# One more group solved whole on VectorE, its Y turned without TensorE, and the weights' low parts subtracted on GpSimd

## The chip, the cores and the metric

The kernel runs on one core of one Trainium2 chip. The metric is the device time of one execution in microseconds (us). Three timed executions of the kernel before took 637.04 to 637.57 us, with a median of 637.5 us.

A core has five engines that run side by side and wait for one another through semaphores: PE (TensorE, matrix products and the loading of their weights), DVE (VectorE), ACT (ScalarE), POOL (GpSimd) and SP (here only the DMA issues). Each engine takes its own instructions strictly in the order in which the program lists them.

## The reference

A linear-attention recurrence (a delta rule) over 768 tokens, for 4 batches of 8 heads of size 48, feeds a gated two-layer network:

```python
k_n = k / (norm(k) + 1e-6)
for t in range(768):
    y[t] = q[t] @ state
    state = state + b[t] * outer(k_n[t], v[t] - state.T @ k_n[t])   # per batch and head
x = y.transpose(0, 2, 1, 3).reshape(3072, 384)
out = (sigmoid(x @ w_gate) * (x @ w_val)) @ w_out                   # 384 -> 1536 -> 384
```

Everything is float32, and the products of the network are made of pairs of narrower parts: each weight and each activation is split into a high part in a narrower float (fp32r) and a low part, the remainder.

## The kernel before

**Groups.** The 768 tokens are cut into 12 groups (g = 0 to 11) of 64 tokens. For one group and all 32 heads the recurrence becomes block algebra. Step by step:

- `gram` (L282): PE multiplies the keys with each other (`pg`); ACT copies the blocks out into `G` and `L`.
- `norms` (18 short DVE instructions): the norms of the keys and the factors `gam` and `mq` from the diagonal of `G`. `scale_v` (ACT, L279) scales V.
- The solve: a triangular 32 x 32 system for each of the chunks. `solve` (L329) does it whole on DVE: 31 pairs of a multiply (L347) and an add (L350), and a 32 x 32 transposition into `mt` (L352). `solve_halves` (L373) solves two 16 x 16 halves on DVE (15 pairs, L392 and L395) and joins them on PE with 64 small products `pz` and 64 small products `pm` (both L409), a DVE transposition (L422), an ACT copy (L423) and a DVE subtraction (L430); it needs `joint` (a cleared tile, GpSimd) and `lower_left` (ACT). Groups 0, 1 and 2 use the halves, the groups from 3 on the whole solve.
- `rest`, `updates` (three steps), `rows`, `advance`: PE products with the running state `su`, with ACT and DVE moving the results out of PSUM. `rows` leaves the group's Y in `ys`.
- Y has to be turned (tokens along the free axis) and split into `xh` and `xl` (the high and the low part of x) before the network can use it. `flip` (L533, groups 0 to 2) does it on PE (three transpositions `pt` for each half, L542), with ACT (L547) for the high and DVE (L548) for the low part. `turn` (L551, groups from 3 on) uses one DVE transposition (`yt`, L557), sixteen block copies, eight on GpSimd and eight on ACT (L562), one ACT cast for `xh` (L571) and one DVE subtraction for `xl` (L573).

**The network.** For each group and each f = 0 to 11: `gate_val` (PE, 24 products of both weights; L583 for group 0 in full float32, L586 with split parts from group 1 on), `gated` (ACT sigmoid L591, DVE multiply L592), `split_hi` and `split_lo` (ACT L597, DVE L602), and `outp` (PE, L611 or L617) two tiles later. From group 1 on, the products of `gate_val` go in the order high times high, high weight times `xl`, low weight times `xh`; so the second product of a group needs `xl`.

**The weights.** 36 weight pieces (three for each f) come in over DMA as 64-bit words, are put together (ACT L189 and L191, DVE L203) and split for the groups from 1 on: `weight_hi` (ACT cast, L212) writes the high part, `weight_lo` (DVE, L219) the low part. Memory is reused: the tile that `weight_hi` of an odd piece n writes is the one whose old content `weight_hi` and `weight_lo` of the pieces n - 3 and n - 2 read, so the odd cast n waits for the low part n - 2.

**The order.** `slot(s)` (L811) writes the order by hand. An even slot is a `gate_val` and an odd one an `outp`; 24 slots are one group of the network. In each slot run, in this order: the products, what the table `plan` holds for it, the split or the gating, what `late` holds, and what `tail` holds (the weight splits). Group g + 1 is solved and updated in the slots of group g. A tile below is called by group and f: (1,9) is `gate_val` of group 1 with f = 9 and what belongs to it, in slot 24 + 18 = 42.

Of the kernel before, what the change touches and what calls it, by code (L numbers as in the profile page):

```python
# [12 lines left out]
F32 = mybir.dt.float32  # L13
# [6 lines left out]
ALU = mybir.AluOpType  # L20
# [11 lines left out]
CP = 2 * J  # L32
# [23 lines left out]
def deltanet_gated_mlp(ctx: ExitStack, tc: tile.TileContext, kd, qd, kv, beta, words, out):  # L56
    nc = tc.nc
# [4 lines left out]
    wk = ctx.enter_context(tc.tile_pool(name="wk", bufs=1))  # L62
# [18 lines left out]
    joints = {0: scratch, 1: scratch}  # L81
# [25 lines left out]
    def load_q(g, after=None):  # L107
        for e in range(2):
            ins = nc.sync.dma_start(kqp[g % 2][64 * e:64 * e + 64, 2 + e:4 + e].rearrange("p s c t -> p (s c t)"), qd[g, e])
            pace(ins, after)  # L110
# [104 lines left out]
    def weight_lo(n):  # L215
        f, w = pieces[n]
        t, u = parts[w, f]
        parts[w, f] = t
        nc.vector.tensor_tensor(out=t[:, 1], in0=u, in1=t[:, 0].bitcast(F32), op=ALU.subtract)  # L219

    def joining():
        for n in range(len(pieces)):
# [88 lines left out]
    def masked(g):  # L311

        kq = kqp[g % 2]
        pool, tag = (ps_aux, "aux") if g else (ps_out, "po")
        pp = [pool.tile([128, J, C], F32, name=f"pp_{g}_{e}", tag=tag) for e in range(2)]
        for j in range(J):
            for e, x in KINDS:
                r, t = 64 * e, tokens_at(e, x)
                nc.tensor.matmul(out=pp[e][t:t + 64, j], lhsT=kq[r:r + D, x, j], rhs=kq[r:r + D, 3 if x else 2 + 2 * e, j], start=True, stop=True)  # L319

        def masks():
            for e, x in sorted(KINDS):
                t, sec = tokens_at(e, x), 5 if x else 2 + 2 * e
                nc.vector.tensor_tensor(out=kq[t:t + 64, sec], in0=pp[e][t:t + 64],  # L324
                                        in1=pmask[t:t + 64, e].unsqueeze(1).to_broadcast([64, J, C]), op=ALU.mult)
                yield
        return masks()
# [27 lines left out]
    def lower_left(g):  # L355

        if g == 0:
            for r in range(4):
                q, o = slice(32 * r, 32 * r + 32), 32 * (r % 2)
                nc.scalar.activation(wide[q, :, o:o + 16].rearrange("q c t -> q t c"), state[g]["G"][q, 0:16], AF.Copy, scale=under[q])  # L360
            return
        a = joints[g][:, 0]
        return nc.scalar.activation(a[:, :, 0:16].rearrange("q c t -> q t c"), state[g]["G"][:, 0:16], AF.Copy, scale=under)

    def joint(g):
        joints[g] = wk.tile([128, 3, CP, 32], F32, name=f"scratch_{g}", tag=f"xx{(g + 1) % 2}", bufs=1)
        nc.gpsimd.memset(joints[g][:, 0], 0.0)

    def clear(g):
        state[g]["X"] = X = wk.tile([128, 16, 32], F32, name=f"X_{g}", tag="X", bufs=1)  # L370
        nc.gpsimd.memset(X, 0.0)
# [258 lines left out]
    plan = collections.defaultdict(list)  # L630
    late = collections.defaultdict(list)

    def steps(gen, n=1):
        def fn():
            for _ in range(n):
                next(gen, None)
        return fn

    def spread(gen, total, lo, hi, room=lambda s: 1.0, into=plan):

        done, upto, whole = 0, 0.0, sum(room(s) for s in range(lo, hi))
        for s in range(lo, hi):
            upto += total * room(s) / whole
            n = total if s == hi - 1 else round(upto)
            into[s].append(steps(gen, n - done))
            done = n

    def chain(*gens):
        for q in gens:
            yield from q  # L650

    def take(gen, n=1):
        for _ in range(n):
            next(gen, None)

    def scaling(g, s):
        for i in range(4):
            plan[s + i].append(steps(scalings[g], 4))

    scalings = [scale_v(g) for g in range(N)]  # L660
    NORMS, SOLVE, HALVES = 18, 66, 40
# [78 lines left out]
    for part in (1, 0):  # L740
        plan[{1: 6, 0: 11}[part]].append(lambda part=part: load_rows(2, part))
    plan[13].append(lambda: load_q(2))
    halves2 = solve_halves(2)
    plan[12].append(lambda: clear(2))
    plan[23].append(lambda: joint(2))
    plan[24].append(lambda: lower_left(2))

    busy = collections.Counter()

    def mask_later(g, s):  # L750
        def fn():
            masks = masked(g)
            take(masks, 2)
            plan[s + 1].insert(0, steps(masks, 2))
        late[s].append(fn)
        for i in range(2):
            busy[s + i] += 1.4

    def gram_later(g, s):
        def fn():  # L760
            copies = gram(g)
            for i, n in enumerate((4, 2, 4) if g < 4 else (6, 4)):
                plan[s + 1 + i].append(steps(copies, n))
        late[s].append(fn)

    solves = []
    for g in range(N):
        w = W * (g - 1)
        if g == 0:
            late[3].append(lambda: advance(0))  # L770
            continue
        up, at_rows = (13, 19) if g < 3 else (9, 15)
        at_rest = {1: 8, 2: 28}.get(g, w + 6)
        late[at_rest].append(lambda g=g: rest(g))
        for step in range(3):
            late[w + up + 2 * step].append(lambda g=g, step=step: updates(g, step))
        late[w + at_rows].append(lambda g=g: rows(g))
        if g > 2:
            turned = turn(g)
            late[w + at_rows].append(steps(turned))  # L780
        late[w + at_rows].append(lambda g=g: advance(g))
        if g < 3:
            for c in range(2):
                late[w + at_rows + 2].append(lambda g=g, c=c: flip(g, c))
                busy[w + at_rows + 2] += 0.6
        else:
            for at, n in ((16, 3), (17, 3), (18, 2), (19, 1), (20, 1)):
                late[w + at].append(steps(turned, n))
            busy[w + 15] += 0.6
            busy[w + 20] += 0.6  # L790
        busy[at_rest] += 1.1
        busy[w + up + 2] += 1.1
        busy[w + at_rows] += 1.1
        busy[w + at_rows + 1] += 1.1
        if g == 1:
            mask_later(1, 14)
        else:
            if g > 2:
                plan[w - 27].append(lambda g=g: load_group(g))
            gram_later(g, {2: 3, 3: 32}.get(g, w - 18))  # L800
            mask_later(g, {2: 25, 3: 38}.get(g, w - 13))
            if g > 2:
                solves.append((g, w - 13 if g == 3 else w - 15, w + 8))
            scaling(g, {2: 25, 3: 43}.get(g, w - 4))
    spread(chain(norms(2), halves2), NORMS + 36, 8, 25, lambda s: max(0.1, 1.6 - busy[s]))
    for at in (26, 29, 30, 30, 31):
        plan[at].append(steps(halves2))
    for g, lo, hi in solves:
        spread(chain(norms(g), solve(g)), NORMS + SOLVE, lo, hi, lambda s: max(0.1, 1.6 - busy[s]))

# [71 lines left out]
```

## Time and profile before

| what | value |
|---|---|
| median of three timed runs | 637.5 us |
| the profiled execution's own time | 635.61 us |
| its span, first to last instruction | 633.9 us |
| PE busy | 614.6 us (97%) |
| DVE busy | 476.8 us (75%) |
| ACT busy | 344.0 us (54%) |
| POOL busy | 39.6 us (6%) |
| granted TensorE clock | 0.998 of full |

The profile shows one execution. Line numbers are those of the kernel before. An instruction's row gives its start, its duration, its engine and line, what it writes and reads, and in brackets how long the engine stood idle just before it and what ended that idle time. Durations of instructions that follow each other on an engine overlap a little, so the distance from start to start is shorter than the printed duration.

### The profile page before, as it was taken

What the parts mean: (1) busy time and instruction counts of PE and PEld (TensorE: products, weight loads), DVE (VectorE), ACT (ScalarE), POOL (GpSimd) and SP (SyncE); (2) the same over time, 40 slices, a digit from 0 to 9 for tenths busy, and PEclk for the clock granted to TensorE, in tenths of its full rate; (3) what the DMA queues carried; (4) which work ended last, traced back from release to release, by engine and by line L of the source; (5) the groups of instructions that cost most, each with busy time, mean ns of one, the idle gap of its engine ahead of it and who ended that gap; (6) DMA issues with size and microseconds to landing.
All of it is one profiled execution on the core that took longest, in us unless ns stands there. A gap on an engine that the chain in (4) does not pass through costs nothing.

```text
span 633.9 us, 24057 instructions
## 1 busy us (share of the span) xinstructions
PE 614.6 (97%) x10494; PEld 571.2 (90%) x10502; DVE 476.8 (75%) x1443; ACT 344.0 (54%) x933; POOL 39.6 (6%) x102
## 2 busy tenths in 40 slices
PE   6689999999999999999999999999999999999996
PEld 4367778989999999999999999999999999999996
DVE  5888897589977977977977977977987977953221
ACT  4879865567356356356355355355455455445222
POOL 6000000000002002002002002002002002001000
PEclk9999999999999999999999999999999999999999
DMA  9495831202203203103102102102112100100101
GB/s 271 177 296 181 277 91 54 53 2 87 52 3 86 52 4 86 42 12 86 45 11 86 34 21 87 27 28 86 26 29 86 26 4 3 26 3 2 26 1 25
DMA packets 17769, 41.06 MB, mean 65 GB/s; under 512 B 4224, under 2 KB 7296, under 8 KB 17664
## 3 DMA queue, kind: packets, MB, share of 16 engines
q1 hardware_dynamic: 17664, 39.53, 21.5%
q8 instruction: 82, 1.34, 0.9%
q14 instruction: 23, 0.19, 0.1%
HBM read 34.80 MB, written 4.72 MB: 62 GB/s over the span
## 4 chain that ended last, share of the span: by engine, by line
PE 91%; DVE 5%; ACT 1%; issue 1%; DMA 1%; ACTq 0%; SPq 0%; DVEq 0%
PE gv L586 45%; PE po L617 22%; PE gv L583 5%; PE pu L477 3%; PE po L611 3%; PE yy L503 2%; PE yy L506 2%; PE pk L446 2%; PE pg L291 2%; PE pp L319 2%; PE pd L524 2%; PE pk L469 1%; PE pm L409 1%; ACT su L483 1%; DVE kqp L324 1%
## 5 line engine op out<-in xcount | busy, mean ns | idle before, releaser
L586 PE MATMUL gv<-xx,w 128*128 128x256 f32 x2376 | 311.2, 285 | 0.0
L586 PEld LDWEIGHTS gv<-xx,w 128*128 128x128 f32 x2376 | 298.8, 191 | 3.1
L617 PE MATMUL po<-w,h 128*128 128x384 f32 x792 | 161.9, 340 | 0.0
L617 PEld LDWEIGHTS po<-w,h 128*128 128x128 f32 x792 | 133.8, 188 | 0.8
L597 ACT CAST h<-sg 128x256 fp32r<-128x256 f32 x132 | 53.5, 405 | 120.1 <-DVE sg L592 119.0
L591 ACT ACTIVATE sg<-gv 128x256 f32<-128x256 f32 x144 | 54.7, 380 | 107.8 <-PE gv L586 98.5
L592 DVE TENSOR_TENSOR sg<-sg,gv 128x256 f32<-128x256 f32 x144 | 60.1, 417 | 67.3 <-ACT sg L591 66.5
L350 DVE TENSOR_TENSOR X<-X,tmp 128x126 f32<-128x126 f32 (+22 forms) x279 | 71.1, 255 | 8.3
L347 DVE TENSOR_TENSOR tmp<-X,gp 128x126 f32<-128x126 f32 (+22 forms) x279 | 71.0, 254 | 8.3
L602 DVE TENSOR_TENSOR h<-sg,h 128x256 fp32r<-128x256 f32 x132 | 56.4, 428 | 13.2 <-ACT h L597 13.2
L562 POOL COPY x<-yt 32x192 f32<-32x192 f32 x72 | 28.3, 393 | 450.3 <-DVE yt L557 447.6
L279 ACT ACTIVATE kv<-kv,mq 128x48 f32<-128x48 f32 x192 | 47.9, 324 | 0.0
L483 ACT COPY su<-pu 32x384 f32<-32x384 f32 x92 | 43.3, 470 | 5.9 <-PE pu L477 4.1
L583 PE MATMUL gv<-xx,u 128*128 128x256 f32 x144 | 33.8, 385 | 0.7 <-issue 0.4
L324 DVE TENSOR_TENSOR kqp<-pp,pmask 64x512 f32<-64x512 f32 x48 | 32.3, 687 | 2.1 <-PE pp L319 1.1
L303 ACT COPY G<-pg 32x256 f32<-32x256 f32 (+1 forms) x69 | 25.3, 367 | 14.0 <-PE pg L291 12.7
L583 PEld LDWEIGHTS gv<-xx,u 128*128 128x128 f32 x144 | 26.6, 190 | 5.8 <-issue 0.8
L557 DVE STREAM_TRANSPOSE yt<-ys 128x768 f32<-128x768 f32 x9 | 8.8, 979 | 25.4 <-ACT ys L512 25.4
L457 DVE TENSOR_TENSOR R<-kv,pk 128x384 f32<-128x384 f32 x44 | 22.3, 549 | 6.6 <-PE pk L469 6.5
L562 ACT COPY x<-yt 32x192 f32<-32x192 f32 x72 | 25.2, 349 | 1.2
L212 ACT CAST w<-u 128x384 fp32r<-128x384 f32 x36 | 18.0, 508 | 8.1 <-DVE w L219 8.0
L531 DVE TENSOR_TENSOR su<-su,pd 48x384 f32<-48x384 f32 x40 | 21.7, 543 | 0.8 <-PE pd L524 0.4
(109 smaller groups left out, 556.2 us busy)
## 6 DMA issues: line engine op xcount, KB each, us to landing
raw<-in_words_dram SPq DMA_DIRECT2D x36, 384.0 KB, 5.5
kv<-in_kv_dram SPq DMA_DIRECT2D x24, 384.0 KB, 4.5
kqp<-in_qd_dram SPq DMA_DIRECT2D x24, 256.0 KB, 4.1
kqp<-in_kd_dram SPq DMA_DIRECT2D x24, 192.0 KB, 3.5
out_dram<-ot SPq DMA_DIRECT2D x48, 96.0 KB, 2.2
beta<-in_beta_dram SPq DMA_DIRECT2D x12, 16.0 KB, 4.0
```

What stands on the lines that cost most here:

```text
L279: nc.scalar.activation(V[:, c], V[:, c], AF.Copy, scale=mq[:, c, 0:1])
L347: nc.vector.tensor_tensor(out=tmp, in0=X[:, k:16, j:j + 1].to_broadcast([128, n, j]), in1=gp[:, j:j + 1, 0:j].to_broadcast([128, n, j]), o ...
L350: nc.vector.tensor_tensor(out=X[:, k:16, 0:j], in0=X[:, k:16, 0:j], in1=tmp, op=ALU.add)
L483: nc.scalar.copy(su[r:r + 32, 3 if x else e], pu[0][r:r + 32])
L562: copy(x[32 * q:32 * q + 32, :, :, a].rearrange("q k c s -> q c k s"), yt[32 * a:32 * a + 32, :, q::4])
L583: nc.tensor.matmul(out=pg[:, o], lhsT=parts[w, f][:, k * 128:(k + 1) * 128], rhs=x[0][:, k], start=k == 0, stop=k == KC - 1)
L586: nc.tensor.matmul(out=pg[:, o], lhsT=parts[w, f][:, a, k * 128:(k + 1) * 128], rhs=x[b][:, k], start=(k == 0 and q == 0), stop=(k == KC - ...
L591: nc.scalar.activation(h, st["gv", f][:, 0], AF.Sigmoid)
L592: nc.vector.tensor_tensor(out=h, in0=h, in1=st["gv", f][:, 1], op=ALU.mult)
L597: nc.scalar.copy(hh[:, 0], st["sg", f])
L602: nc.vector.tensor_tensor(out=hh[:, 1], in0=st["sg", f], in1=hh[:, 0].bitcast(F32), op=ALU.subtract)
L617: nc.tensor.matmul(out=po[s], lhsT=hh[:, a, ts], rhs=parts["o", f][:, w], start=(f == 0 and q == 0), stop=(f == NF - 1 and q == 2))
```

## The change

Three things. `weight_lo` runs on GpSimd instead of DVE, for all 36 pieces. Group 2 is solved by `solve` in place of `solve_halves`, over the slots 8 to 33; its cleared tile, its `lower_left` and the 128 small PE products go away. Group 2's Y is turned by `turn` in place of `flip`, and its updates and rows stand two slots earlier (35, 37, 39 and 41 in place of 37, 39, 41 and 43). A few steps of groups 2 and 3 move by one or two slots with it.

```diff
@@ weight_lo
-        nc.vector.tensor_tensor(out=t[:, 1], in0=u, in1=t[:, 0].bitcast(F32), op=ALU.subtract)
+        nc.gpsimd.tensor_tensor(out=t[:, 1], in0=u, in1=t[:, 0].bitcast(F32), op=ALU.subtract)
...
-    def joint(g):
-        joints[g] = wk.tile([128, 3, CP, 32], F32, name=f"scratch_{g}", tag=f"xx{(g + 1) % 2}", bufs=1)
-        nc.gpsimd.memset(joints[g][:, 0], 0.0)
...
-    halves2 = solve_halves(2)
-    plan[12].append(lambda: clear(2))
-    plan[23].append(lambda: joint(2))
-    plan[24].append(lambda: lower_left(2))
...
-        up, at_rows = (13, 19) if g < 3 else (9, 15)
+        up, at_rows = {1: (13, 19), 2: (11, 17)}.get(g, (9, 15))
...
-        if g > 2:
+        if g > 1:
             turned = turn(g)
             late[w + at_rows].append(steps(turned))
...
-        if g < 3:
+        if g < 2:
             for c in range(2):
                 late[w + at_rows + 2].append(lambda g=g, c=c: flip(g, c))
...
-            for at, n in ((16, 3), (17, 3), (18, 2), (19, 1), (20, 1)):
-                late[w + at].append(steps(turned, n))
+            for at, n in ((1, 3), (2, 3), (3, 2), (4, 1), (5, 1)):
+                late[w + at_rows + at].append(steps(turned, n))
...
-            gram_later(g, {2: 3, 3: 32}.get(g, w - 18))
-            mask_later(g, {2: 25, 3: 38}.get(g, w - 13))
-            if g > 2:
-                solves.append((g, w - 13 if g == 3 else w - 15, w + 8))
-            scaling(g, {2: 25, 3: 43}.get(g, w - 4))
-    spread(chain(norms(2), halves2), NORMS + 36, 8, 25, lambda s: max(0.1, 1.6 - busy[s]))
-    for at in (26, 29, 30, 30, 31):
-        plan[at].append(steps(halves2))
+            gram_later(g, {2: 3, 3: 31}.get(g, w - 18))
+            mask_later(g, {2: 25, 3: 36}.get(g, w - 13))
+            solves.append((g, *{2: (8, 34), 3: (35, 56)}.get(g, (w - 15, w + 8))))
+            scaling(g, {2: 24, 3: 44}.get(g, w - 4))
```

What this does to the order is seen at three places. The numbers at the end of a tile's name only tell tiles apart; `w_35` is weight piece 35, `sg_1_10` belongs to tile (1,10). The changed file is four lines shorter from `joint` on, so L558 there is L562 here, L567 is L571, L569 is L573, and L587, L588, L593 and L598 are L591, L592, L597 and L602.

ACT, in the last slots of the network's group 1, before:

```order
L279 ACTIVATE kv_3_1706<-kv_3_1706,mq_3_2495 128x48 x4
L597 CAST h_1_9_2616<-sg_1_9_2596 128x256
L512 COPY ys_2_2668<-yy_2_0_2618 128x8x48
L512 COPY ys_2_2668<-yy_2_1_2619 128x8x48
L279 ACTIVATE kv_3_1706<-kv_3_1706,mq_3_2495 128x48 x4
L591 ACTIVATE sg_1_10_2737<-gv_1_10_2710 128x256
L279 ACTIVATE kv_3_1706<-kv_3_1706,mq_3_2495 128x48 x4
L597 CAST h_1_10_2761<-sg_1_10_2737 128x256
L547 CAST xx_2_2763<-pt_2_0_2764 128x3x128
L547 CAST xx_2_2763<-pt_2_1_2770 128x3x128
L279 ACTIVATE kv_3_1706<-kv_3_1706,mq_3_2495 128x48 x4
L591 ACTIVATE sg_1_11_2807<-gv_1_11_2776 128x256
```

and now, from behind the sigmoid of tile (1,9) and three block copies on:

```order
L212 CAST w_34_2599<-u_17_1586 128x384
L212 CAST w_35_2602<-u_17_1586 128x384
L593 CAST h_1_9_2618<-sg_1_9_2583 128x256
L558 COPY x_2_2586<-yt_2_2519 32x2x3x32 x3
L279 ACTIVATE kv_3_1705<-kv_3_1705,mq_3_2439 128x48 x4
L587 ACTIVATE sg_1_10_2655<-gv_1_10_2624 128x256
L558 COPY x_2_2586<-yt_2_2519 32x2x3x32 x2
L279 ACTIVATE kv_3_1705<-kv_3_1705,mq_3_2439 128x48 x4
L593 CAST h_1_10_2687<-sg_1_10_2655 128x256
L567 CAST xx_2_2518<-x_2_2586 128x768
L279 ACTIVATE kv_3_1705<-kv_3_1705,mq_3_2439 128x48 x4
L587 ACTIVATE sg_1_11_2720<-gv_1_11_2690 128x256
```

The block copies of `turn(2)` and its cast to `xh` now stand between the sigmoids; the last two weight casts stand behind the first three block copies.

POOL, in the same slots, where before there were only clears and the block copies of groups from 3 on:

```order
L219 TENSOR_TENSOR w_31_2450<-u_15_1493,w_31_2450 128x384
L219 TENSOR_TENSOR w_32_2453<-u_16_1510,w_32_2453 128x384
L558 COPY x_2_2586<-yt_2_2519 32x2x3x32 x8
L219 TENSOR_TENSOR w_33_2560<-u_16_1510,w_33_2560 128x384
L219 TENSOR_TENSOR w_34_2599<-u_17_1586,w_34_2599 128x384
L219 TENSOR_TENSOR w_35_2602<-u_17_1586,w_35_2602 128x384
```

The low part of piece 33, for which the cast of piece 35 waits, stands behind the eight block copies.

DVE, before, between the gating of tiles (1,10) and (1,11):

```order
L592 TENSOR_TENSOR sg_1_10_2737<-sg_1_10_2737,gv_1_10_2710 128x256
L347 TENSOR_TENSOR tmp_3_24_2759<-X_3_2497,gp_3_2254 128x96
L548 TENSOR_TENSOR xx_2_2763<-pt_2_0_2764,xx_2_2763 128x3x128
L548 TENSOR_TENSOR xx_2_2763<-pt_2_1_2770,xx_2_2763 128x3x128
L350 TENSOR_TENSOR X_3_2497<-X_3_2497,tmp_3_24_2759 128x4x24
```

and now, at the gating of tile (1,11):

```order
L347 TENSOR_TENSOR tmp_3_21_2717<-X_3_2441,gp_3_2165 128x126
L598 TENSOR_TENSOR h_1_10_2687<-sg_1_10_2655,h_1_10_2687 128x256
L588 TENSOR_TENSOR sg_1_11_2720<-sg_1_11_2720,gv_1_11_2690 128x256
L569 TENSOR_TENSOR xx_2_2518<-x_2_2586,xx_2_2518 128x768
L350 TENSOR_TENSOR X_3_2441<-X_3_2441,tmp_3_21_2717 128x6x21
```

The low part of group 2's x was made behind the gating of (1,10); it is now made behind the gating of (1,11), the last tile ahead of the first that uses it.

## Rows read from the trace of the kernel before

**Rows 1.** The page: busy time of each engine in us (share of the span, instructions).

```profile
PE 614.6 (97%) x10494; PEld 571.2 (90%) x10502; DVE 476.8 (75%) x1443; ACT 344.0 (54%) x933; POOL 39.6 (6%) x102
```

**Rows 2.** Busy time of each engine in three stretches: tiles (0,5) to (0,11), the tiles of group 1, those of group 2. After the stretch come its length and, for each engine, busy us (instructions); then clock, DMA share and GB/s.

```profile
63.60:101.20 37.60, 37.05 (x669) 28.65 (x663) 32.16 (x94) 25.78 (x58) 0.53 (x1) 1.00 0.58 176
101.20:157.70 56.50, 55.09 (x1158) 50.74 (x1157) 44.27 (x120) 37.40 (x106) 0.00 (x0) 1.00 0.14 40
157.70:205.85 48.15, 48.15 (x834) 46.53 (x834) 40.05 (x125) 25.03 (x71) 3.18 (x8) 1.00 0.17 46
```

**Rows 3.** The chain of waits, in order of time (start us, us, what), around the joining products and around the transpositions of group 2.

```profile
114.30 1.22 PE pz L409 x82
115.52 2.34 PE gv L586 x18
117.86 0.48 PE pm L409 x38
118.35 0.26 issue
118.61 0.95 PE pm L409 x62
119.56 1.24 PE po L617 x6
120.81 2.15 PE gv L586 x18
...
152.78 1.05 PE po L617 x6
153.83 0.66 PE pt L542 x6
```

**Rows 4.** The two longest idle times of PE in group 1, in its timeline (start us, us, instruction, and in brackets the idle time before it and its end).

```profile
135.98 1.15 PE L319 MATMUL pp<-kqp 48*64 48x64 f32 x62 [0.83 <-ACT su L483]
147.36 1.14 PE L503 MATMUL yy<-su,kqp 48*64 48x48 f32 x62 [0.31 <-ACT su L483]
```

**Rows 5.** ACT and DVE ahead of those two idle times, and the page's group of the weight casts (busy us, mean ns, idle us before them and what ended most of it).

```profile
133.58 0.41 ACT L597 CAST h<-sg 128x256 fp32r<-128x256 f32 x1 [0.70 <-DVE sg L592]
144.96 0.41 ACT L597 CAST h<-sg 128x256 fp32r<-128x256 f32 x1 [1.50 <-DVE sg L592]
...
L212 ACT CAST w<-u 128x384 fp32r<-128x384 f32 x36 | 18.0, 508 | 8.1 <-DVE w L219 8.0
```

**Rows 6.** GpSimd beside DVE: its only subtraction (early, with DVE idle), its block copies in group 3 (all eight, then the second, and the one that met L336), and DVE at the same instants; the last two lines are DVE's L336 and L602 in a place where GpSimd rests.

```profile
3.73 1.26 POOL L141 TENSOR_TENSOR mr<-mr 128x512 f32<-128x512 f32 x1
193.52 3.47 POOL L562 COPY x<-yt 32x192 f32<-32x192 f32 x8 [92.51 <-DVE yt L557]
193.90 0.34 POOL L562 COPY x<-yt 32x192 f32<-32x192 f32 x1
193.90 0.56 DVE L531 TENSOR_TENSOR su<-su,pd 48x384 f32<-48x384 f32 x1
195.80 0.71 POOL L562 COPY x<-yt 32x192 f32<-32x192 f32 x1
195.60 1.19 DVE L336 SCALAR_TENSOR_TENSOR gp<-gp,gam 128x512 f32<-128x512 f32 x2
196.70 0.56 DVE L602 TENSOR_TENSOR h<-sg,h 128x256 fp32r<-128x256 f32 x1
...
143.24 1.02 DVE L336 SCALAR_TENSOR_TENSOR gp<-gp,gam 128x512 f32<-128x512 f32 x2
144.17 0.42 DVE L602 TENSOR_TENSOR h<-sg,h 128x256 fp32r<-128x256 f32 x1
```

**Rows 7.** DVE: the low parts of the weights in group 1's stretch (a group: busy us, mean ns), three of them in a row, and one form of the whole solve's pairs over the run.

```profile
L219 DVE TENSOR_TENSOR w<-u,w 128x384 fp32r<-128x384 f32 x27 | 14.1, 552 | 0.0
123.75 1.49 DVE L219 TENSOR_TENSOR w<-u,w 128x384 fp32r<-128x384 f32 x3
L347 DVE TENSOR_TENSOR tmp<-X,gp 128x96 f32<-128x96 f32 x18 | 4.6, 258 | 0.6
```

**Rows 8.** The turn of group 3 in the timelines: first three `gate_val` of PE (the first one behind the rows of group 3, the next, and the first tile of the network's group 3), then ACT and DVE; the last line is the page's group of the gating multiply (busy us, mean ns, idle us before).

```profile
192.71 2.42 PE L586 MATMUL gv<-xx,w 128*128 128x256 f32 x18
196.03 2.33 PE L586 MATMUL gv<-xx,w 128*128 128x256 f32 x18
205.69 2.33 PE L586 MATMUL gv<-xx,w 128*128 128x256 f32 x18
195.23 0.38 ACT L591 ACTIVATE sg<-gv 128x256 f32<-128x256 f32 x1 [2.79 <-PE gv L586]
195.64 1.07 ACT L562 COPY x<-yt 32x192 f32<-32x192 f32 x3
199.68 0.71 ACT L562 COPY x<-yt 32x192 f32<-32x192 f32 x2
200.79 0.83 ACT L571 CAST xx<-x 128x768 fp32r<-128x768 f32 x1
201.52 1.01 ACT L279 ACTIVATE kv<-kv,mq 128x48 f32<-128x48 f32 x4
203.17 0.95 DVE L573 TENSOR_TENSOR xx<-x,xx 128x768 fp32r<-128x768 f32 x1
...
L592 DVE TENSOR_TENSOR sg<-sg,gv 128x256 f32<-128x256 f32 x144 | 60.1, 417 | 67.3 <-ACT sg L591 66.5
```

More of the change, by code (lines that the diff above doesn't have):

```diff
@@ L786, in deltanet_gated_mlp @@
         else:
-            for at, n in ((16, 3), (17, 3), (18, 2), (19, 1), (20, 1)):
-                late[w + at].append(steps(turned, n))
-            busy[w + 15] += 0.6
-            busy[w + 20] += 0.6
+            for at, n in ((1, 3), (2, 3), (3, 2), (4, 1), (5, 1)):
+                late[w + at_rows + at].append(steps(turned, n))
+            busy[w + at_rows] += 0.6
+            busy[w + at_rows + 5] += 0.6
         busy[at_rest] += 1.1
```

## The prediction

> **What bounds the kernel now.** I read the page's busy times first: PE is busy for 614.6 of 633.9 us, 97% [rows 1]. Then the windows by stretch [rows 2]. From the network's group 2 on PE is busy in every microsecond (48.15 of 48.15), so nothing outside PE matters there. The change touches the two stretches before that: tiles (0,5) to (0,11), where PE idles 0.55 us of 37.6, and the tiles of group 1, where it idles 1.41 us of 56.5. In both, time is gained mainly by taking products off PE, and lost where PE is made to wait. DVE has 37.6 - 32.16 = 5.4 us free in the first and 56.5 - 44.27 = 12.2 us in the second. Third I read the chain of waits, where the joining products and the transpositions of group 2 stand in PE's own row with nothing beside them that ends later [rows 3]. Last come the timelines around PE's idle times [rows 4, 5] and around GpSimd's copies [rows 6].
>
> **Products taken off PE.** Gone are `pz` 1.22 us, and `pm` 0.48 + 0.26 + 0.95 = 1.69 us with its wait. The `gv` behind `pz` takes 2.34 us and the `po` behind `pm` 1.24, where others take 2.15 and 1.05: another 0.19 + 0.19. The transpositions `pt` take 0.66. Together 3.95 us [rows 3]. All of it lies on the path, since PE bounds the stretch.
>
> **Old idle times of PE.** `pp` waited 0.83 us and the rows' products 0.31 us for ACT's copies of `su` [rows 4]. Each time ACT had stood still just before its copies, for a gating multiply of DVE that was late: 0.70 and 1.50 us [rows 5]. DVE's queue there held norms, masks, R and three low parts for each tile. With the low parts gone from it I take both waits as gone, 1.14 us; at the other end they stay, 0. The gain is then 5.1 us, at least 3.95.
>
> **DVE's work.** In group 1's stretch 27 low parts leave it [rows 7]; from start to start they take (1.49 - 0.55) / 2 = 0.47 us each, 12.7 us. The order shows what else changes there: 19 more pairs of L347 and L350 come in, 38 at about 0.26 us [rows 7], 9.9, with one transposition more for Y (about 1, twice the elements of a 0.5 us subtraction) and one for `mt` against one; 11 short instructions of the halves, two transpositions, the subtraction L430 and two L548 go, which I put at 5 us from their sizes. So DVE's busy time falls from 44.3 to about 38 us, if nothing slows it down. In the stretch before, nine low parts go (4.2 us) and some 2 us come in: 32.2 becomes about 30.
>
> **GpSimd's work.** Its one subtraction has 512 columns and took 1.26 us [rows 6]; by size 384 columns are 0.95, and a copy of 192 columns takes 0.34, so with a fixed part I take 0.97. In group 1's stretch 27 are 26 us of 56, so GpSimd itself is not full, and the pieces are cast some six steps ahead of their use: PE does not wait for a weight. What GpSimd reads it reads beside DVE. In group 3 a copy took 0.34 us beside L531, which has one input in PSUM; one that met L336, with both inputs in SBUF, took 0.71. L336 took 1.19 for the pair of it in place of 1.02, and L602 0.56 in place of 0.42 [rows 6]. So beside such an instruction each waits for the other, here by 0.14 to 0.37 us; how much for a longer subtraction no row shows. Bounds for the loss of DVE per subtraction: 0, when GpSimd finds DVE idle or at work on PSUM, and 0.97, when DVE has only two-input work. A bit over half of DVE's remaining work is two-input work (pairs, norms, L602), so I take 0.5. That is 13.5 us in group 1's stretch: 38 + 13.5 = 51.5, against PE's own 55.09 - 3.95 = 51.1 with the old idle time gone. DVE is then as full as PE, but may lag by up to two `gv` tiles before PE feels it. I charge 0.3 us for it and keep 0 and the upper end for the range. In the stretch before, 30 + 9 x 0.5 = 34.5 stays below 37.6: nothing.
>
> The Trainium skill (SBUF — State Buffer, Who interferes with whom) says that a VectorE instruction with two SBUF inputs and a GpSimd instruction that reads SBUF exclude each other, and that the second one blocks until the first has ended. The rows above agree in kind. By that rule at its hardest every subtraction would cost DVE its full length; this is the third case below.
>
> **The new wait: xl of group 2.** Before, `xl` was made behind the gating of (1,10); now it stands on DVE behind the gating of (1,11), and only one `outp` lies between that tile's `gv` and the first `gv` of group 2, whose second product needs `xl`. Group 3's turn has the same steps with one tile more [rows 8]. I take its times and set t = 0 at 192.71, where the first `gv` behind the rows begins. PE reaches the tiles at 0, 3.32, then every (205.69 - 196.03) / 3 = 3.22 us: the first tile of group 2 is the fourth, at 9.76.
> GpSimd's block copies run from 0.81 to 4.28 [rows 6], and the low part of piece 33 behind them to 5.3.
> ACT: the sigmoid of (1,9) at 2.52, three block copies to 4.0, the cast of piece 34 to 4.4. The cast of piece 35 must wait for the low part of 33, until 5.3, and ends at 5.8. Behind it stand a cast of h 0.4, three block copies 1.0, four scalings 0.9: the sigmoid of (1,10) starts near 8.1, though its `gv` was ready at 5.6. Then that sigmoid 0.3, two block copies 0.65, four scalings 0.9, a cast of h 0.3, the cast `xh` 0.8, four scalings 0.9: the sigmoid of (1,11) starts near 12.0, the gating multiply near 12.4 and, 0.35 later, `xl` (0.95), which ends at 13.7. (Durations from [rows 5, 8], less some 0.1 for the overlap of neighbours.)
> PE needs it at 9.76 + 0.12, after one product. It waits 3.8 us; I take 3.7. Lower bound: group 3's own `xl` ended at 204.12, 1.57 us before PE needed it, with one tile of 3.22 more, so 3.22 - 1.57 - 0.12 = 1.5 us, without the weight casts and four more scalings. Upper bound 5: DVE's lag on top. What makes it late is the place of the rows: slot 41 is seven slots ahead of group 2's first `gate_val`, while group 3's rows stand nine slots ahead of theirs.
>
> **The rest.** Two casts and `lower_left` on ACT go, the block copies come; ACT has 19 us free in the stretch [rows 2], and where its lateness counts it is in the sum above. The waits of ACT for the low parts, 8 us in all [rows 5], change their releaser; GpSimd starts each low part as soon as the cast is done, so they should shrink to half a microsecond each, hidden under `gv`. The cleared tile and its memset cost nothing on an idle GpSimd. SP issues the same transfers in the same order.
>
> **Sum.** -3.95 - 1.14 + 3.7 + 0.3 = -1.1 us. The profiled execution took 635.61 us, so it would be 634.5; the median of the timed runs lies 1.9 us above the profiled one, and the forecast for them is 637.5 - 1.1 = 636.4 us.
>
> **The rivals.**
> *xl comes in time.* If ACT is not held by piece 35 and its queue runs as in group 3, the wait is 1.5 us or less: -5.1 + 1.5 = -3.6, 633.9 us. For it: group 3's margin of 1.57 us. Against: ACT has four scalings and two casts more there, in order ahead of the sigmoid.
> *Given back in full.* The old waits stay, because ACT's queue is late for another reason, and `xl` is late by 4: -3.95 + 4 = 0, 637.5 us.
> *GpSimd and DVE block each other.* Slower than before. Place: the pairs L347 and L350 in tiles (1,0) to (1,4) and (1,10), where a low part meets two-input work on end. Price: from 38 + 27 x b = 56.5, or b = 0.68 us lost per subtraction, DVE needs more than the whole stretch took. At b = 0.8 it needs 59.6, so +3.1 us and 640.6; with the full 0.97, 64.2 and +7.7. For it: every two-input row near a copy of GpSimd was longer [rows 6]. Against: DVE's idle time and its work on PSUM (masks, R, `su`, gating) take a good part of the overlaps.
>
> **How the numbers follow.** A measurement of this kernel tells 0.2%, 1.3 us, from no change. The forecast has 0.43 (its own range 634.9 to 638.1), of which 0.19 falls under 636.2 and 0.24 within 1.3 us of 637.5. `xl` in time has 0.22, all faster. Given back has 0.13, of which 0.11 the same and 0.02 slower. Blocking has 0.22, 0.21 slower and 0.01 the same. So faster 0.41, the same 0.36, slower 0.23. The range leaves out the further half of the blocking case and a little below: 633.4 to 640.6.
>
> **What would show it.** Right: no L409 or L542 of group 2 on PE; a PE idle time of 3 to 4 us at the second product of the first group 2 tile, ended by L569 on DVE; ACT's cast of piece 35 waiting some 1 us for L219 on GpSimd; the 0.83 and 0.31 us gone. Each subtraction near 0.97 us on GpSimd, longer beside the pairs. Wrong: no wait at that tile; or idle times of PE in tiles (1,1) to (1,8) that a late gating ends, with L347 and L350 above 0.5 us beside L219. The forecast falls if the low parts on GpSimd take over 1.4 us each, or if ACT waits for them by more than 10 us in all.

## The result and the profile after

The changed kernel takes 640.43 us (median of 6 runs, 639.08 to 642.7); the kernel before, run beside it, takes 636.63. The ratio over all runs is 1.0068, 95% interval 1.0047 to 1.009: slower by 0.7%, where the forecast was 1.1 us faster. The time lies just inside the upper end of the range (640.6). Runs of one kernel differ by up to some 7 us. One reason shows in the profiles: the first gating product of TensorE starts at 42.09 us in that of before and at 44.50 in that of after, where the two programs are still the same; between 38.2 and 41.5 us the granted clock is 1.00 in the first and 0.50 in the second. So medians are compared, and stretches inside a trace by their length. Three slow executions far from all others (668 us of the kernel before, 839 of e5, 1173 of e11) are left out of every number below.

The page's busy times of after, and its group of the low parts (busy us, mean ns, idle us before them and what ended most of it):

```profile
PE 616.5 (96%) x10240; PEld 570.7 (89%) x10240; DVE 487.9 (76%) x1434; ACT 345.8 (54%) x938; POOL 79.5 (12%) x144
...
L219 POOL TENSOR_TENSOR w<-u,w 128x384 fp32r<-128x384 f32 x36 | 38.0, 1072 | 87.2 <-ACT w L212 79.2
```

PE has fewer products than in [rows 1] and yet is busy for longer. DVE gave 36 subtractions away and is busier by 11.1 us. Now the same three windows as in [rows 2], in the same columns:

```profile
63.60:101.20 37.60, 36.80 (x783) 28.22 (x782) 34.19 (x83) 26.86 (x61) 10.92 (x10) 1.00 0.62 178
101.20:157.70 56.50, 53.28 (x903) 48.73 (x902) 52.14 (x116) 35.58 (x99) 30.02 (x34) 1.00 0.15 39
157.70:205.85 48.15, 44.34 (x783) 42.19 (x783) 36.85 (x112) 22.19 (x61) 3.19 (x8) 0.93 0.18 46
```

The program of after stands 2.5 us later in these windows. In the first window DVE went from 32.16 to 34.19 us and PE idles 0.80 us, as before nearly. In group 1's window DVE went from 44.27 to 52.14 us; from the start of the first tile of group 1 to that of group 2, wherever these lie in the trace, the view says the same:

```profile
103.71:159.78 56.07, 51.16 (x894) 46.86 (x892) 52.21 (x118) 36.86 (x103) 30.02 (x34) 1.00 0.15 40
```

In the third window of the table, where PE had been busy in every microsecond, it now stands still for 3.81 us, and the granted clock is 0.93. The waits of PE between 60 and 210 us (what waits, for whom, us in total, times, longest):

```profile
PE gv L582 <- DVE xx L569: 2.1, 1, 2.1
PE pu L473 <- ACT sg L587: 1.8, 1, 1.8
PE gv L582 <- DVE tmp L347: 1.7, 1, 1.7
PE po L613 <- DVE h L598: 1.4, 1, 1.4
```

Four waits, 7.0 us. The two of [rows 4] are gone. The view names ACT for the second, but `pu` needs `mt`, and DVE's timeline shows what made that late. The last line but one is ACT's copies of `L`, the first two of which free the PSUM tile that `pu` writes (start us, us, instruction):

```profile
125.32 0.19 DVE L347 TENSOR_TENSOR tmp<-X,gp 128x30 f32<-128x30 f32 x1
...
125.60 3.05 POOL L219 TENSOR_TENSOR w<-u,w 128x384 fp32r<-128x384 f32 x3 [1.11 <-ACT w L212]
...
126.10 0.67 DVE L350 TENSOR_TENSOR X<-X,tmp 128x30 f32<-128x30 f32 x1
...
126.80 0.93 DVE L347 TENSOR_TENSOR tmp<-X,gp 128x16 f32<-128x16 f32 x1
...
127.76 0.93 DVE L350 TENSOR_TENSOR X<-X,tmp 128x16 f32<-128x16 f32 x1
128.73 0.71 DVE L352 STREAM_TRANSPOSE mt<-X 128x512 f32<-128x512 f32 x1
...
127.57 1.50 ACT L308 COPY L<-pg 32x256 f32<-32x256 f32 x4
...
129.59 0.88 PE L473 MATMUL pu<-R,mt 32*32 32x48 f32 x64 [1.83 <-ACT sg L587]
```

Instructions of a pair that take 0.19 us each alone take 0.67 to 0.93 beside three subtractions of GpSimd. They alternate: one instruction of DVE for each subtraction. Against 0.19 us each the last three lose 2.0 us, and the transposition that makes `mt` comes by so much later. This is not all of the wait: by the rows above the first two copies of `L` end near 128.3, so as an estimate `pu` would have waited some 0.6 us even with `mt` in time.

The turn of group 2 in after, which answers to [rows 8] (the first `gate_val` behind the rows starts at 146.50):

```profile
142.77 3.68 POOL L219 TENSOR_TENSOR w<-u,w 128x384 fp32r<-128x384 f32 x3 [1.60 <-ACT w L212]
142.93 2.65 DVE L336 SCALAR_TENSOR_TENSOR gp<-gp,gam 128x512 f32<-128x512 f32 x2
...
145.51 1.22 DVE L598 TENSOR_TENSOR h<-sg,h 128x256 fp32r<-128x256 f32 x1
...
146.50 2.42 PE L582 MATMUL gv<-xx,w 128*128 128x256 f32 x18
...
147.09 0.41 ACT L593 CAST h<-sg 128x256 fp32r<-128x256 f32 x1 [3.18 <-DVE sg L588]
...
149.34 3.22 POOL L558 COPY x<-yt 32x192 f32<-32x192 f32 x8 [2.89 <-DVE yt L553]
...
152.64 3.00 POOL L219 TENSOR_TENSOR w<-u,w 128x384 fp32r<-128x384 f32 x3
...
153.73 0.52 ACT L212 CAST w<-u 128x384 fp32r<-128x384 f32 x1 [2.76 <-POOL w L219]
...
157.46 0.63 PE L613 MATMUL po<-w,h 128*128 128x384 f32 x2 [1.39 <-DVE h L598]
...
159.78 0.39 PE L582 MATMUL gv<-xx,w 128*128 128x256 f32 x1 [1.70 <-DVE tmp L347]
...
161.28 0.95 DVE L569 TENSOR_TENSOR xx<-x,xx 128x768 fp32r<-128x768 f32 x1
...
162.29 4.00 PE L582 MATMUL gv<-xx,w 128*128 128x256 f32 x17 [2.11 <-DVE xx L569]
```

Read it from the top. L336 took 2.65 us for the pair instead of 1.02 [rows 6], then L598 1.22 instead of 0.42: ACT's cast waited 3.18 us behind them, with the copies of Y in its queue. GpSimd, after 2.89 us of waiting, made its block copies late and the low parts behind them; the cast of piece 35 stood 2.76 us for the first of these, and all of ACT's turn stood behind that cast. PE waited at the last `po` of group 1 and at the first two products of group 2. And then the gating product itself took 4.00 us. The windows (columns as in [rows 2]) say why:

```profile
162.29:166.29 4.00, 4.00 (x18) 4.00 (x19) 3.12 (x11) 0.00 (x0) 0.00 (x0) 0.50 0.00 0
...
168.11:170.25 2.14, 2.14 (x19) 2.14 (x19) 1.93 (x8) 0.00 (x0) 0.00 (x0) 1.00 0.00 0
```

The granted clock was 0.50, the lower level of 1.2 GHz, after three idle times of PE in some six microseconds, and at 2.4 GHz again in the next tile. From the start of that product to the next tile's passed 5.65 us; with the full clock it is 3.19 (163.41 to 166.60 in `e3_warm`, below).

From the start of the first tile of group 1 to that of the second tile of group 2 the kernel before needed 101.19 to 160.74, 59.55 us; after needs 103.71 to 167.94, 64.23. The 4.7 us come out as -3.95 - 1.14 + 7.03 of waits + 2.46 of clock, 4.4, which leaves 0.3 open. From there on PE is full, as before.

### The profile page after: what moved, and what is told of

The parts are those of the page before. It is cut to its first block, busy times and chain, and to the rows that moved or that the text cites. A ratio compares the mean times of both kernels' runs of the same rounds, so it can differ in the third digit from the quotient of the medians.

```text
span 641.0 us, 23601 instructions
## 1 busy us (share of the span) xinstructions
PE 616.5 (96%) x10240; PEld 570.7 (89%) x10240; DVE 487.9 (76%) x1434; ACT 345.8 (54%) x938; POOL 79.5 (12%) x144
## 4 chain that ended last, share of the span: by engine, by line
PE 85%; DVE 7%; ACT 4%; issue 1%; POOL 1%; DMA 1%; ACTq 0%; SPq 0%; DVEq 0%; POOLq 0%
PE gv L582 43%; PE po L613 20%; PE gv L579 3%; PE pu L473 3%; PE pp L319 2%; PE po L607 2%; PE yy L499 2%; PE yy L502 2%; PE pg L291 2%; PE pk L442 2%; PE pd L520 1%; PE pk L465 1%; ACT kv L279 1%; ACT G L303 1%; PE gap L99 1%
## 5 line engine op out<-in xcount | busy, mean ns | idle before, releaser
L587 ACT ACTIVATE sg<-gv 128x256 f32<-128x256 f32 x144 | 54.8, 381 | 118.2 <-PE gv L582 106.3
L593 ACT CAST h<-sg 128x256 fp32r<-128x256 f32 x132 | 53.5, 405 | 118.3 <-DVE sg L588 117.3
L588 DVE TENSOR_TENSOR sg<-sg,gv 128x256 f32<-128x256 f32 x144 | 60.1, 417 | 61.4 <-ACT sg L587 60.6
L347 DVE TENSOR_TENSOR tmp<-X,gp 128x126 f32<-128x126 f32 (+22 forms) x310 | 85.4, 275 | 9.3
L350 DVE TENSOR_TENSOR X<-X,tmp 128x126 f32<-128x126 f32 (+22 forms) x310 | 82.3, 266 | 9.1
L558 POOL COPY x<-yt 32x192 f32<-32x192 f32 x80 | 31.2, 391 | 405.9 <-DVE yt L553 403.0
L598 DVE TENSOR_TENSOR h<-sg,h 128x256 fp32r<-128x256 f32 x132 | 59.0, 447 | 12.9 <-ACT h L593 12.9
L219 POOL TENSOR_TENSOR w<-u,w 128x384 fp32r<-128x384 f32 x36 | 38.0, 1072 | 87.2 <-ACT w L212 79.2
L558 ACT COPY x<-yt 32x192 f32<-32x192 f32 x80 | 27.9, 349 | 1.3
L473 PEld LDWEIGHTS pu<-R,mt 32*32 32x32 f32 x1408 | 16.5, 105 | 8.0 <-ACT sg L587 2.1
```

The costliest lines, as they stand in the source:

```text
L347: nc.vector.tensor_tensor(out=tmp, in0=X[:, k:16, j:j + 1].to_broadcast([128, n, j]), in1=gp[:, j:j + 1, 0:j].to_broadcast([128, n, j]), o ...
L350: nc.vector.tensor_tensor(out=X[:, k:16, 0:j], in0=X[:, k:16, 0:j], in1=tmp, op=ALU.add)
L558: copy(x[32 * q:32 * q + 32, :, :, a].rearrange("q k c s -> q c k s"), yt[32 * a:32 * a + 32, :, q::4])
L587: nc.scalar.activation(h, st["gv", f][:, 0], AF.Sigmoid)
L588: nc.vector.tensor_tensor(out=h, in0=h, in1=st["gv", f][:, 1], op=ALU.mult)
L593: nc.scalar.copy(hh[:, 0], st["sg", f])
```

## The experiments

Three theories stood at first. A: VectorE is full in group 1 whichever engine makes the low parts, because the whole solve came to it, and the turn of group 2, late at its late place, does the rest. L: the mutual blocking of GpSimd and VectorE is the whole cost. P: the late place of `xl` alone is.

**e1, the low parts back on VectorE.**

```diff
-        nc.gpsimd.tensor_tensor(out=t[:, 1], in0=u, ...)
+        nc.vector.tensor_tensor(out=t[:, 1], in0=u, ...)
```

> The whole change, but the low parts of the weights stay on VectorE. Theory A (VectorE is full in group 1 whichever way the low parts are done, since the whole solve came to it, so the turn of group 2 is late at its late place, PE idles and its clock falls): L347 and L350 never above 0.4 us, no wait of ACT for GpSimd, but VectorE carries 27 x 0.47 = 12.7 us more itself; PE still waits 2 to 4 us at the first tile of group 2; 636 to 639 us. Rival L (the mutual exclusion of GpSimd and VectorE alone made the loss): PE's waits go, the products taken off PE are won, 632 to 634 us. Rival P (the late place of xl alone): as the changed kernel, 640 us.

638.58 us, ratio 1.0038 (1.0024 to 1.0053). PE's waits:

```profile
PE gv L582 <- DVE xx L569: 2.1, 1, 2.1
PE gv L582 <- ACT xx L567: 1.2, 1, 1.2
PE pp L319 <- ACT su L479: 1.2, 1, 1.2
PE yy L499 <- ACT su L479: 0.6, 1, 0.6
```

The late turn stays without any subtraction on GpSimd, with the clock at half behind it (4.00 us again), and the old waits of [rows 4] are back, longer. L as the whole cost falls. Here the turn runs as it was forecast: GpSimd's copies start 0.86 us behind the first `gate_val` after the rows and `xl` ends at 13.60, where the prediction had 0.81 and 13.7; in after they came at 2.84 and 15.73.

```profile
143.81 2.42 PE L582 MATMUL gv<-xx,w 128*128 128x256 f32 x18
...
144.67 3.44 POOL L558 COPY x<-yt 32x192 f32<-32x192 f32 x8 [120.36 <-DVE yt L553]
...
156.46 0.95 DVE L569 TENSOR_TENSOR xx<-x,xx 128x768 fp32r<-128x768 f32 x1
```

**e2, the low parts on GpSimd alone**, in the kernel before (the reverse of e1's edit, with solve and flip as they were).

> The kernel before with one line changed: the low parts on GpSimd. Theory A: 27 x 0.47 us leave VectorE in group 1 and about 27 x 0.52 come back as waits for GpSimd, so nothing is left: within 1 us of the kernel before, 636 to 637.5 us; VectorE's pairs beside a subtraction take 0.9 to 1.0 us instead of 0.2 to 0.3. Rival L: most of the 4 us of the loss is here, 639.5 to 641 us. Rival P: as before, 636.5 us, and no wait of PE that was not there.

637.98 us, ratio 1.0038 (1.0016 to 1.006). P as the whole cost falls with this, since `flip` is at its old place here; the time lies between A's range and L's. The two parts nearly add up: 0.38% and 0.38% against 0.68% for both. Here is DVE in the norms, beside three subtractions, and what follows:

```profile
130.30 2.95 POOL L219 TENSOR_TENSOR w<-u,w 128x384 fp32r<-128x384 f32 x3 [0.67 <-ACT w L212]
130.42 0.95 DVE L253 SCALAR_TENSOR_TENSOR ny<-nt,ny 128x32 f32<-128x32 f32 x1
...
131.40 0.93 DVE L249 SCALAR_TENSOR_TENSOR nt<-ny 128x32 f32<-128x32 f32 x1
...
132.36 0.97 DVE L251 TENSOR_TENSOR nt<-nt,gp 128x32 f32<-128x32 f32 x1
133.37 0.19 DVE L253 SCALAR_TENSOR_TENSOR ny<-nt,ny 128x32 f32<-128x32 f32 x1
...
134.51 0.40 ACT L597 CAST h<-sg 128x256 fp32r<-128x256 f32 x1 [3.06 <-DVE sg L592]
...
136.91 1.16 PE L319 MATMUL pp<-kqp 48*64 48x64 f32 x62 [2.48 <-ACT su L483]
```

Instructions of 32 columns, 0.19 us alone, take 0.93 to 0.97: each pays the rest of a subtraction, however short it is itself. The gating multiply queued behind them is late, ACT's cast behind that, and the 0.83 us of [rows 4] become 2.48. (This is the fastest of its twelve runs, with a stretch only 1.0 us longer than before; what the timed ones lose beyond it shows in no row.) In the stretch from the first tile of group 1 to the second of group 2 DVE is busy for 43.91 us, where before it was 47.11 with 26 low parts. At 0.47 us from start to start 12.2 us left with them, so 9.0 came back, 0.35 for each subtraction.

**e3, TensorE kept busy ahead of group 2:** 16 products of 512 columns into an unused PSUM tile before its first gating product.

```diff
+            if s == 2 * W:
+                busy_array(ps_aux.tile([128, J, C], F32, name="warm", tag="aux"), 16)
```

> The changed kernel with 16 products of 512 columns on a constant, into a free PSUM tile, ahead of the first gate_val of group 2, where PE idled for 4 us; they are needed for nothing. Theory A with the clock: at 0.21 us each they lie within the idle time, the granted clock stays at 1.0 where it was 0.5 for 6 us, and 2 to 3 us come back: 637 to 638.5 us. If the clock is not what the slow products behind the wait show: 640 to 641 us, and the first gate_val of group 2 still takes 4 us.

```profile
159.07 3.63 PE L99 MATMUL warm<-dmask 128*128 128x512 bf16 x16
...
163.41 2.30 PE L582 MATMUL gv<-xx,w 128*128 128x256 f32 x17 [0.59 <-DVE xx L569]
```

The gating product takes 2.30 us instead of 4.00, but the kernel is not faster: 641.26 us, ratio 1.0076 (1.005 to 1.0102). In its trace the clock fell at the earlier wait on `pu` instead, where the gating product behind it took 3.63 us. The expectation missed, though the slow product behind `xl` was the clock: with the idle time filled it was gone. Filling this one didn't pay; the wait on `pu` was as long in after (1.83 us, here 1.86) and left the clock alone there.

**e4, the turn of group 2 two slots earlier**, as group 3's stands, with the fourth group's Gram products, masks and solve a slot or two earlier with it.

```diff
-        up, at_rows = {1: (13, 19), 2: (11, 17)}.get(g, (9, 15))
+        up, at_rows = {1: (13, 19)}.get(g, (9, 15))
```

> The changed kernel with group 2's updates and rows two slots earlier (33 to 39 in place of 35 to 41), its solve ending by slot 32, group 3's gram and masks one slot earlier: xl then stands behind the gating of tile (1,10), as in the later groups. The low parts stay on GpSimd. Theory A: the waits at the first tile of group 2 (1.4 + 1.7 + 2.1) and the 2.8 us of low clock mostly go, a wait for mt of 2 to 4 us stays or grows: 634.5 to 637.5 us. Rival L: VectorE is as late as before, so the waits only move: 639 us and more. Rival P: 632.5 to 634.5 us.

637.59 us, ratio 1.0027 (1.0007 to 1.0046), 0.4% below after and just above A's range. The wait for `xl` is gone. What remains, with 3.91 us for the gating product behind the first of the two:

```profile
PE pu L473 <- ACT L L308: 2.3, 1, 2.3
PE po L613 <- DVE h L598: 1.9, 1, 1.9
```

So neither part alone is the cause. The second batch asks what holds VectorE: its own work, or what GpSimd reads.

**e5, e4 with the low parts on VectorE.**

> The turn of group 2 two slots earlier, as in e4, and the low parts on VectorE, as in e1: the second group's whole solve, its turn off TensorE and no GpSimd subtraction in one kernel. Theory A (VectorE is full in group 1's stretch whichever engine does the low parts, since a subtraction costs it about 0.5 us either way): VectorE's busy time between 101 and 157 us stays at 50 to 52 us, TensorE keeps waits of 3 to 4 us in group 1, and the time is 635 to 637.5 us, within 0.3% of the kernel before. Rival L (it was the mutual exclusion of GpSimd and VectorE that kept e4 from its gain): 632 to 634.5 us.

635.64 us, ratio 1.0005 (0.9983 to 1.0028): as A has it, no gain, and rival L falls. DVE's busy time between 101 and 157 us is 50.72.

**e6, GpSimd writes the low half and reads nothing.**

```diff
-        nc.gpsimd.tensor_tensor(out=t[:, 1], in0=u, in1=t[:, 0].bitcast(F32), op=ALU.subtract)
+        nc.gpsimd.memset(t[:, 1].bitcast(F32), 0.0)
```

> The changed kernel with one edit: GpSimd fills each low half with zeros instead of subtracting (the low parts of the weights are left out of the computation; the semaphores and the order stay). It tells whether VectorE is held by what GpSimd reads. If the holding comes with the two inputs that GpSimd reads: L347's and L350's products of group 1 stay near 0.3 us beside GpSimd, VectorE's busy time between 103.7 and 159.8 us falls from 52.2 to 38 to 40 us, the wait of TensorE on pu goes, the chain of the turn comes 3 us earlier, and the time is 632.5 to 635.5 us (below the kernel before). If writing alone holds VectorE too, or if GpSimd isn't what holds it (theory: VectorE's own instructions fill the stretch), the busy time stays above 48 us and the time at 638 to 641 us.

636.38 us, ratio 1.0011 (0.9991 to 1.0031). Two of DVE's costliest lines between 101 and 157 us (instructions, busy us, mean ns, idle us), after first and then e6:

```profile
L347 DVE TENSOR_TENSOR tmp<-X,gp 128x120 f32<-128x120 f32 (+20 forms) x26 | 11.7, 448 | 0.8
L598 DVE TENSOR_TENSOR h<-sg,h 128x256 fp32r<-128x256 f32 x10 | 6.6, 658 | 0.0
```

```profile
L347 DVE TENSOR_TENSOR tmp<-X,gp 128x126 f32<-128x126 f32 (+22 forms) x31 | 8.0, 257 | 0.9
...
L598 DVE TENSOR_TENSOR h<-sg,h 128x256 fp32r<-128x256 f32 x11 | 4.6, 419 | 0.3 <-ACT h L593 0.3
```

With the writing left in and the reading gone, L347 falls from 448 to 257 ns in the mean and L598 from 658 to 419, its length alone. The twelve tiles of group 1 have 38.90 us of DVE instead of 52.21: 13.3 us for 26 subtractions, 0.51 each.

```profile
102.29:154.13 51.84, 51.14 (x894) 47.07 (x892) 38.90 (x119) 36.69 (x103) 11.84 (x31) 1.00 0.17 43
```

My 38 to 40 us came; the time was too low by 0.9 us, since the turn stays late:

```profile
PE gv L582 <- DVE xx L569: 2.1, 1, 2.1
...
PE gv L582 <- ACT xx L567: 0.5, 1, 0.5
```

The memset also takes only 0.42 us where a subtraction takes 1.02, so ACT's casts come sooner for that reason too; the kernel doesn't separate the two. For DVE's durations that doesn't matter: L347's mean beside it is what it is alone (0.26 us, [rows 7]).

**e7, the whole solve alone:** low parts on VectorE, Y turned by `flip` on TensorE at the place of before.

```diff
-        up, at_rows = {1: (13, 19), 2: (11, 17)}.get(g, (9, 15))
+        up, at_rows = (13, 19) if g < 3 else (9, 15)
...
-        if g > 1:
+        if g > 2:
             turned = turn(g)
...
-        if g < 2:
+        if g < 3:
```

> Only the whole solve of the third group: low parts on VectorE and the group's Y still turned on TensorE, as in the kernel before. Theory A (VectorE's load by the whole solve is the cost): the products that joined the halves go (3.95 us less on TensorE in the sum of the prediction), but VectorE has 5 to 7 us more to do in group 1's stretch and is full, TensorE waits there for 2 to 4 us, 634.5 to 637.5 us. Rival T (the late turn with its six extra instructions is the whole cost, the solve is free): 632 to 634 us.

635.1 us, ratio 0.9991 (0.9969 to 1.0013). A's range holds: no gain from the whole solve as placed. One wait of 2.59 us on `pu` stands in its trace, until VectorE had made masks of the fourth group, and the gating product behind it took 3.92 us. Three of its twelve runs took 632.4 to 632.8 us, so that cost may not be in every run. Against e1 (1.0038) the turn and its place cost 0.47%, 3.0 us.

**e8, both reliefs:** e4 with GpSimd only writing.

> e4 (turn of group 2 two slots earlier, low parts on GpSimd) with GpSimd filling the low halves with zeros instead of subtracting (the low parts of the weights are left out). If GpSimd's reading is what holds VectorE, nothing is left that stops TensorE's gain of 5 us: 631 to 633 us. If VectorE's own instructions fill the stretch: 636 to 638 us, as e4.

631.94 us, ratio 0.9945 (0.9926 to 0.9964), a gain of 3.5 us. In its trace the stretch from the first tile of group 1 to the second of group 2 is 54.63 us, 4.9 below before: nearly the 5.1 that the prediction had counted ahead of its losses. From e4 to e8 0.82%, from after to e6 0.57%: what GpSimd reads costs 3.6 to 5.2 us, less whatever part the shorter instruction has in it. That is against no subtraction at all; made on VectorE it costs nearly as much (e1, e5).

The last three kernels ask whether what is left without GpSimd is a few late waits that a placement removes.

**e9, e5 with the fourth group's Gram products one slot earlier** (`3: 30` to `3: 29` in `gram_later`).

> e5 (turn two slots earlier, low parts on VectorE) with the fourth group's Gram products one slot earlier (29), so that ScalarE's copies of its L free the PSUM tile before TensorE's pu wants it. In e5's trace that wait was 1.97 us and the gate products behind it ran 0.2 us longer. If what is left of the cost is single late waits that a placement removes: the pu wait goes and the time falls by 1.5 to 2.5 us against e5, to 633.5 to 635 us, just below the kernel before. If VectorE being full moves the wait on to the next consumer: 635.5 to 637 us, as e5.

635.02 us, ratio 0.9992 (0.9977 to 1.0008). The 2.0 us wait on `pu` shrank to 0.3, but at three other places PE now waits 0.5 to 0.9 us; the gain on e5 is 0.13%, inside the intervals, and the time falls between the two ranges.

**e10, e7 with the fourth group's masks one slot earlier.**

```diff
-            mask_later(g, {2: 25, 3: 36}.get(g, w - 13))
+            mask_later(g, {2: 25, 3: 35}.get(g, w - 13))
```

> e7 (the whole solve alone, Y still turned on TensorE, low parts on VectorE) with the fourth group's masks one slot earlier (35), so that VectorE reads pp before TensorE's pu wants its PSUM tile. In e7's trace that wait was 2.59 us and the next gate products ran 3.92 instead of 2.2 us at a granted clock of half. If single late waits are what is left: 631 to 633.5 us, 2 to 4 us below the kernel before. If VectorE being full moves the wait on: 634.5 to 636 us, as e7.

632.64 us (five runs, 632.39 to 634.77), ratio 0.9954 (0.9941 to 0.9967): faster than both kernels, with the whole computation in it. The tiles of group 1 in its trace (columns as in [rows 2]) and the longest waits of PE from 60 to 200 us:

```profile
103.44:156.72 53.28, 52.42 (x900) 48.14 (x899) 49.12 (x142) 35.54 (x102) 0.00 (x0) 1.00 0.15 42
```

```profile
PE yy L499 <- ACT su L479: 0.4, 1, 0.4
PE pk L465 <- ACT su L479: 0.2, 1, 0.2
```

DVE is as full as in after, 49.12 of 53.28 us (92%) against 52.21 of 56.07 (93%), and PE idles 0.86 us instead of 4.91. Theory A in its plain form falls with this: a VectorE as full as that is no loss in itself. What is lost depends on which instruction is late in it.

**e11, e9 with the low parts on GpSimd.**

> e9 with the low parts on GpSimd, the one difference between the two. If a subtraction costs VectorE the same on either engine (0.55 us of its own against about 0.5 us held): within 1 us of e9. If GpSimd's holding costs TensorE more than the plain instruction does, because it comes in the middle of VectorE's chains and ScalarE waits about 1.0 instead of 0.55 us for each low part: 1 to 2.5 us more than e9.

635.41 us, ratio 1.0006 (0.9991 to 1.002), 0.14% above e9 with intervals that overlap. At this place the engine of the subtraction makes no measurable difference; in the late turn it made 0.30% (after against e1).

## Why the prediction was wrong, step by step

*Products off TensorE, -3.95.* The products are gone from the trace, and the gain is real: e10, which keeps the transpositions `pt`, and e8 end 2.9 and 3.5 us below the kernel before. In the changed kernel it was there and was given back.

*The old idle times, -1.14.* Gone in after, as written, but not for the reason given. The reason was that the low parts leave DVE's queue; in e2 they leave it and the wait on `pp` grows from 0.83 to 2.48 us. In after `pu` and `pp` stand two slots earlier.

*DVE's load.* The forecast was 38 + 27 x 0.5 = 51.5 us; the window shows 52.14. The 38 are 38.90 in e6, and the loss per subtraction, a guess of 0.5 between 0 and 0.97, is 0.35 by e2 and 0.51 by e6. In the stretch before, 34.5 was forecast and 34.19 came, without a loss. GpSimd's time was taken as 0.97; it is 1.02 at the median and up to 1.47. So the sizes were right, though no row stood behind the 0.5, and they already said that the move frees nothing: a subtraction costs VectorE 0.47 us from start to start where VectorE makes it, and 0.51 where GpSimd does in this kernel. With the low parts on VectorE (e1) the tiles of group 1 have 50.31 us of DVE, and 52.21 without.

*The charge for it, 0.3 us: this step failed.* I wrote that DVE "may lag by up to two `gv` tiles before PE feels it", and compared two sums, 51.5 of DVE and 51.1 of PE. A sum can't tell it. The loss doesn't come spread out at 0.5 us; it comes as 0.75 us on each of several short instructions in a row (the end of a solve, the norms), and a chain that PE waits for lies behind them. The trace shows 1.83 us at `pu`, most of it for this, and the 3.18 us of ACT at the start of the turn. The blocking isn't needed for a lag: e1 has none and PE waits 1.2 + 0.6 us in group 1 all the same, at `pp` and `yy`.

*The wait for xl, 3.7 us: right place, too small.* PE's wait that L569 ends is there as described, with 1.39 and 1.70 us ahead of its 2.11: 5.20. The chain itself was timed rightly: in e1, where no subtraction blocks DVE, `xl` ends at 13.60 and PE idles 3.36 us. In after the same chain starts 2.0 us late, at the blocked L336 and L598, and ends 2.1 us later than in e1; ACT's wait for the low part of piece 33, taken as 1 us, was 2.76. I had put DVE's lag into the upper bound of 5 only.

*The clock, not in the sum: this step failed too, and is the largest.* 2.46 us more. No row of before shows an idle time of PE with slower products behind it, and I put no price on one.

Lag, `xl` and clock make 1.83 + 5.20 + 2.46 = 9.5 us where the sum had 4.0. That the time still lies in the range is luck: its upper end came from a rival at b = 0.8, and nothing was lost at that rate. The rival "GpSimd and DVE block each other" gave 640.6 us, and its signs came: L347 and L350 above 0.5 us beside L219, waits in group 1 besides that of `xl`. But it put its turning point at b = 0.68, where DVE's sum passes the stretch, and the kernel lost at 0.51. It named a mechanism that is there, with the wrong condition, and only part of the cost: e1 loses 0.38% without it. "Xl in time" fell; that the whole solve would fit beside a VectorE at 91% was right, by e10, but only with the masks at another place.

The rule of the Trainium skill (SBUF — State Buffer, Who interferes with whom) that was weighed as the hard case, an exclusive lock between two-input instructions of VectorE and GpSimd, agrees with e2's rows: 0.95 us for an instruction of 0.19. Beside e6's memset, which reads nothing, such instructions keep their own length.

What stays open: how much of e6's and e8's gain comes from the shorter instruction on GpSimd, and at which of PE's idle times the clock falls.

## What to carry to other kernels

Before giving VectorE's elementwise work to an idle GpSimd, compare what VectorE saves with what it loses to the blocking: here 0.47 against 0.35 (e2) to 0.51 us (after) for one subtraction of 128x384, so little or nothing was freed. Price a nearly full engine by the chains that run through it and not by its sum: a VectorE that was busy for 92 to 93% of group 1 cost PE 0.9 us of waits in e10 and 4.9 in after, and one slot for a mask (e7 and e10) made 1.7 us of waits. Time a moved chain on the engine's load at its new place, and add the slower products behind each wait that TensorE gets.

## What was not expected of the hardware

A stream of subtractions on GpSimd lets one two-input instruction of VectorE through for each, and that one is charged the rest of the subtraction: 0.93 to 0.97 us for 32 columns in e2. So the shortest instructions lose the most for their length: they take five times as long, while L598 (0.42 alone) went to 1.24 at most.

The clock fell to half behind some idle times of TensorE and not behind others: 4.00 us for the gating product behind 1.39 + 1.70 + 2.11 us of idle time in after, 3.92 behind a single 2.59 in e7, and 3.63 behind 1.86 in e3, but 2.29 behind 0.51 + 2.12 in e6, and 2.42 behind 1.97 in e5. Idle times of one length went both ways: 1.86 in e3 and 1.83 in after, both at `pu`, left 3.63 and 2.40 us. The runs don't tell what decides it.
